# A GEGLU feed-forward kernel whose GELU is computed by one ScalarE activation and one VectorE multiply instead of seven operations

## The chip, the cores and the metric

The kernel runs on one core of a Trainium2 chip. Times are device microseconds (us) of one execution; the *span* in a profile is from the first to the last instruction and is about 2 us shorter than the time. Engines: PE is TensorE, PEld its weight loads, ACT is ScalarE, DVE is VectorE, SP issues most transfers. PSUM is the memory that matmuls accumulate into; a bank is one of its 8 buffers of 128x512 here. The granted clock is the share of TensorE's full clock that the profile records. A run is of the slow state when it took over 1.5% more than the fastest of its kernel; unless a state is named, compared runs are of the fast state.

## The reference

```python
B, S, D, F = 32, 32, 1024, 3584            # bf16; x is 1024 x 1024, the weights 1024 x 3584 and 3584 x 1024
def reference(x, w_gate, w_up, w_down):
    return (gelu_tanh(x @ w_gate) * (x @ w_up)) @ w_down
```

## The kernel before

F is cut into 28 slices `ft` of 128, the 1024 tokens into two blocks of 512. The *first stage* makes, for each of the 56 tiles (128 of F by 512 tokens), a gate and an up accumulation of 8 matmuls each, in one PSUM bank each; all 8 banks rotate. The elementwise work turns each pair of banks into a tile of `gT`. The *second stage* multiplies `gT` by `w_down`: 17 accumulations of 28 matmuls.

```python
FC = 4; KQ = DT // 4                        # DT = 8
pspool = ctx.enter_context(tc.tile_pool(name="psum", bufs=8, space=PSUM))
ework  = ctx.enter_context(tc.tile_pool(name="ework", bufs=3))
...
def mm1(ps, wt, t0, tw, d0=0, d1=DT):       # one accumulation of the first stage
    for dt in range(d0, d1):
        nc.tensor.matmul(ps, lhsT=wt[:, dt, :], rhs=xT[:, dt, t0 : t0 + tw],
                         start=(dt == 0), stop=(dt == DT - 1))

def eltwise(ft, t0, tw, gate_ps, up_ps):    # gelu(g) written as g * sigmoid(g * (C2 + C2A * g * g))
    h = ework.tile(...)
    nc.scalar.activation(h, gate_ps, ACT.Copy)
    sq = ework.tile(...)
    nc.scalar.activation(sq, gate_ps, ACT.Square)
    w = ework.tile(...)
    nc.vector.tensor_scalar(w, sq, _C2A, _C2, ALU.mult, ALU.add)
    z = ework.tile(...)
    nc.vector.tensor_tensor(z, w, h, ALU.mult)
    s = ework.tile(...)
    nc.scalar.activation(s, z, ACT.Sigmoid)
    hu = ework.tile(...)
    nc.vector.tensor_tensor(hu, h, up_ps, ALU.mult)
    nc.vector.tensor_tensor(gT[:, ft, t0 : t0 + tw], hu, s, ALU.mult)
...
# head: the first four tiles are accumulated together, quarter by quarter of D as the weights arrive,
#       so that they hold all 8 banks; then the other 52 tiles one after the other
# second stage: out_ps[128 tokens, 512] = sum over ft of gT[:, ft].T @ wd[:, ft]; VectorE evicts, ScalarE's queue stores
```

Of the kernel before, what the change touches and what calls it, by code (L numbers as in the profile page):

```python
# [8 lines left out]
ACT = mybir.ActivationFunctionType  # L9
ALU = mybir.AluOpType  # L10

_C2 = 2.0 * 0.7978845608028654
_A = 0.044715
_C2A = _C2 * _A
# [3 lines left out]
def kernel(  # L18
# [8 lines left out]
    nc = tc.nc  # L27
    P = nc.NUM_PARTITIONS
    fp32 = mybir.dt.float32
    bf16 = mybir.dt.bfloat16  # L30
# [10 lines left out]
    NB = min(N, MM_N)  # L41
# [20 lines left out]
    ework = ctx.enter_context(tc.tile_pool(name="ework", bufs=3))  # L62
# [5 lines left out]
    gT = gpool.tile([P, FT, N], bf16, name="gT")  # L68
# [55 lines left out]

    def eltwise(ft, t0, tw, gate_ps, up_ps):
        h = ework.tile([P, NB], bf16, name="h", tag="h")[:, :tw]
        nc.scalar.activation(h, gate_ps, ACT.Copy)  # L127
        sq = ework.tile([P, NB], bf16, name="sq", tag="sq")[:, :tw]
        nc.scalar.activation(sq, gate_ps, ACT.Square)  # L129
        w = ework.tile([P, NB], bf16, name="w", tag="w")[:, :tw]  # L130
        nc.vector.tensor_scalar(w, sq, _C2A, _C2, ALU.mult, ALU.add)  # L131
        z = ework.tile([P, NB], bf16, name="z", tag="z")[:, :tw]
        nc.vector.tensor_tensor(z, w, h, ALU.mult)  # L133
        s = ework.tile([P, NB], bf16, name="s", tag="s")[:, :tw]
        nc.scalar.activation(s, z, ACT.Sigmoid)  # L135
        hu = ework.tile([P, NB], bf16, name="hu", tag="hu")[:, :tw]
        nc.vector.tensor_tensor(hu, h, up_ps, ALU.mult)  # L137
        nc.vector.tensor_tensor(gT[:, ft, t0 : t0 + tw], hu, s, ALU.mult)  # L138

    def pair(tw):  # L140
        return (
# [4 lines left out]
    def mm1_and_eltwise(ft, t0, tw):  # L146
        ps = pair(tw)
        for p, wt in zip(ps, weights_of(ft)):
            mm1(p, wt, t0, tw)
        eltwise(ft, t0, tw, *ps)  # L150
# [16 lines left out]
    with tc.manual_schedule(engines={mybir.EngineType.PE}):  # L167
        for _ in range(NWARM):
            nc.tensor.matmul(warm_ps, lhsT=ones_w, rhs=ones_m, start=True, stop=True)  # L169
        for dt in range(KQ):  # L170
            for half in range(2):
                hw = HALF * P
                tp = pspool.tile([P, hw], bf16, name="tp", tag="acc")
                for b in range(HALF):
                    nc.tensor.transpose(  # L175
                        tp[:, b * P : (b + 1) * P],
                        x_nat[:, half * HALF + b, dt * P : (dt + 1) * P],
                        ident,
                    )
                dst = xT[:, dt, half * hw : (half + 1) * hw]  # L180
                if half == 0:
                    nc.vector.tensor_copy(dst, tp)  # L182
                else:
                    nc.scalar.copy(dst, tp)  # L184
        nc.tensor.matmul(warm_ps[:, : NB // 2], lhsT=ones_w, rhs=ones_m[:, : NB // 2], start=True, stop=True)
        head = [pair(NB) for _ in range(FC)]
        for q in range(3):
            for which in (0, 1):
                for dt in range(q * KQ, (q + 1) * KQ):
                    for ft in range(FC):  # L190
                        mm1(head[ft][which], weights_of(ft)[which], 0, NB, dt, dt + 1)
        for ft in range(FC):
            for which in (0, 1):
                mm1(head[ft][which], weights_of(ft)[which], 0, NB, 3 * KQ, DT)
            eltwise(ft, 0, NB, *head[ft])
# [66 lines left out]
```

## Time and profile before

| | before |
|---|---|
| time | 300.71 us (median of 2, 300.66 to 300.75) |
| span of the profiled run | 298.2 us, granted TensorE clock 0.999 |
| PE / DVE / ACT busy | 98% / 37% / 33% |
| rate of matmuls with 512 columns | 216 ns from one to the next, in both stages |

From the profile's page of the kernel before: the busy line and the chain of waits that ended last. Some records of matmuls are missing (1361 of 1387), so PE's true share is nearer 99%.

```profile
PE 292.8 (98%) x1361; PEld 134.4 (45%) x1387; DVE 108.9 (37%) x243; ACT 98.1 (33%) x172; POOL 0.7 (0%) x6
...
PE 96%; DMA 2%; issue 1%; ACTq 0%; DVE 0%
PE out_ps L212 32%; PE up_ps L117 32%; PE gate_ps L117 32%; DMA wu<-in_w_up_dram 2%; ACTq L96 0%; ACTq L80 0%; DVE o_sb L220 0%
```

The chain has no ACT work and no DVE work of the first stage. Its DMA share is one early wait for weights.

The cost groups of the same kernel (busy us in all, mean ns of one, idle time of that engine just before them and what ended it):

```profile
L117 PE MATMUL up_ps<-xT,wu 128*128 128x512 bf16 x440 | 105.6, 379 | 0.5
...
L127 ACT ACTIVATE h<-gate_ps 128x512 bf16<-128x512 f32 x56 | 33.4, 597 | 52.3 <-PE gate_ps L117 51.4
L135 ACT ACTIVATE s<-z 128x512 bf16<-128x512 bf16 x56 | 35.3, 630 | 46.1 <-DVE z L133 46.1
L131 DVE TENSOR_SCALAR w<-sq 128x512 bf16<-128x512 bf16 x56 | 16.5, 295 | 74.6 <-ACT sq L129 74.5
L137 DVE TENSOR_TENSOR hu<-h,up_ps 128x512 bf16<-128x512 bf16 x56 | 38.1, 681 | 12.0 <-ACT h L127 11.9
...
L129 ACT ACTIVATE sq<-gate_ps 128x512 bf16<-128x512 f32 x56 | 33.1, 592 | 0.0
L138 DVE TENSOR_TENSOR gT<-hu,s 128x512 bf16<-128x512 bf16 x56 | 23.8, 426 | 9.9 <-ACT s L135 9.9
L133 DVE TENSOR_TENSOR z<-w,h 128x512 bf16<-128x512 bf16 x56 | 23.8, 425 | 1.8
```

Read the last column by engine. PE has next to no idle time; ACT and DVE have a great deal, and it is PE, or each other, that they wait for. The 379 ns of a matmul is its recorded length, not its pace: matmuls overlap. The pace shows in the timeline, here one tile of the steady first stage (start us, length us, engine, line, idle before):

```profile
186.21 1.89 PE L117 MATMUL up_ps<-xT,wu 128*128 128x512 bf16 x8
186.47 0.60 ACT L127 ACTIVATE h<-gate_ps 128x512 bf16<-128x512 f32 x1 [0.86 <-PE gate_ps L117]
186.97 0.59 ACT L129 ACTIVATE sq<-gate_ps 128x512 bf16<-128x512 f32 x1
187.59 0.29 DVE L131 TENSOR_SCALAR w<-sq 128x512 bf16<-128x512 bf16 x1 [1.52 <-ACT sq L129]
...
187.94 1.89 PE L117 MATMUL gate_ps<-xT,wg 128*128 128x512 bf16 x8
188.26 0.68 DVE L137 TENSOR_TENSOR hu<-h,up_ps 128x512 bf16<-128x512 bf16 x1
188.44 0.63 ACT L135 ACTIVATE s<-z 128x512 bf16<-128x512 bf16 x1 [0.88 <-DVE z L133]
189.10 0.43 DVE L138 TENSOR_TENSOR gT<-hu,s 128x512 bf16<-128x512 bf16 x1 [0.16 <-ACT s L135]
...
189.67 1.89 PE L117 MATMUL up_ps<-xT,wu 128*128 128x512 bf16 x8
```

From 186.21 to 187.94 to 189.67: a group of eight starts every 1.73 us, a tile every 3.45 us, whatever ACT and DVE do in between. The Trainium skill ("TensorE: Matmul & The Clock Gate", "Part 2: What happens when you issue a matmul") gives about 216 ns as the gap between matmuls of 512 columns; 1.73 us / 8 = 216 ns agrees. PE keeps the pace that the page gives, so this is taken as PE's limit.

### The profile page before, as it was taken

Reading aid. Unit: us, or ns where it says so; the run is one execution under the profiler, and the core shown is the slowest. Engines: PE = TensorE matmul, PEld = TensorE weight load, DVE = VectorE, ACT = ScalarE, POOL = GpSimd, SP = SyncE. Lnnn points to the kernel's source line nnn. Section 1 sums busy time; section 2 is a strip of 40 time slices with the busy share of each in tenths; the row PEclk is TensorE's granted clock in tenths of the full one; section 3 lists DMA queues with packets and bytes.
Section 4 is the critical chain, followed back from the end, with each engine's and each line's share of the span. In section 5 each row is a group of like instructions: output and inputs, shape, how many; then the busy total and the mean of one; then the engine's idle time right before and its main releaser. Section 6 shows DMA issues by size and latency. Waiting matters only on the chain.

```text
span 298.2 us, 3467 instructions
## 1 busy us (share of the span) xinstructions
PE 292.8 (98%) x1361; PEld 134.4 (45%) x1387; DVE 108.9 (37%) x243; ACT 98.1 (33%) x172; POOL 0.7 (0%) x6
## 2 busy tenths in 40 slices
PE   8999999999999999999999999999999999999996
PEld 3444444444444444444444444444444444444444
DVE  0067654455554445554445555440010001100111
ACT  2087545544544554544554454530000000000000
POOL 0000000000000000000000000000000000000000
PEclk9999999999999999999999999999999999999999
DMA  7999995090026005300800000000001000100001
GB/s 171 317 295 380 387 363 204 0 281 2 0 78 203 2 0 183 98 2 2 279 4 0 0 0 2 0 0 18 20 18 35 18 20 18 35 20 18 18 19 36
DMA packets 28704, 26.43 MB, mean 89 GB/s; under 512 B 8209, under 2 KB 25105, under 8 KB 28689
## 3 DMA queue, kind: packets, MB, share of 16 engines
q1 hardware_dynamic: 25552, 23.60, 25.1%
q10 hardware_dynamic: 3136, 2.62, 2.8%
q8 instruction: 11, 0.18, 0.2%
q14 instruction: 5, 0.03, 0.0%
HBM read 22.28 MB, written 2.10 MB: 82 GB/s over the span
## 4 chain that ended last, share of the span: by engine, by line
PE 96%; DMA 2%; issue 1%; ACTq 0%; DVE 0%
PE out_ps L212 32%; PE up_ps L117 32%; PE gate_ps L117 32%; DMA wu<-in_w_up_dram 2%; ACTq L96 0%; ACTq L80 0%; DVE o_sb L220 0%
## 5 line engine op out<-in xcount | busy, mean ns | idle before, releaser
L117 PE MATMUL gate_ps<-xT,wg 128*128 128x512 bf16 x438 | 105.6, 379 | 0.7
L117 PE MATMUL up_ps<-xT,wu 128*128 128x512 bf16 x440 | 105.6, 379 | 0.5
L212 PE MATMUL out_ps<-wd,gT 128*128 128x512 bf16 (+2 forms) x468 | 96.5, 366 | 0.4
L212 PEld LDWEIGHTS <-gT 128*128 128x128 bf16 x476 | 45.5, 98 | 51.6
L117 PEld LDWEIGHTS <-wu 128*128 128x128 bf16 x448 | 43.8, 98 | 53.2 <-DMA wu<-in_w_up_dram 0.6
L117 PEld LDWEIGHTS <-wg 128*128 128x128 bf16 x448 | 43.8, 98 | 52.9 <-DMA wg<-in_w_gate_dram 0.3
L127 ACT ACTIVATE h<-gate_ps 128x512 bf16<-128x512 f32 x56 | 33.4, 597 | 52.3 <-PE gate_ps L117 51.4
L135 ACT ACTIVATE s<-z 128x512 bf16<-128x512 bf16 x56 | 35.3, 630 | 46.1 <-DVE z L133 46.1
L131 DVE TENSOR_SCALAR w<-sq 128x512 bf16<-128x512 bf16 x56 | 16.5, 295 | 74.6 <-ACT sq L129 74.5
L137 DVE TENSOR_TENSOR hu<-h,up_ps 128x512 bf16<-128x512 bf16 x56 | 38.1, 681 | 12.0 <-ACT h L127 11.9
L220 DVE CAST o_sb<-out_ps 128x512 bf16<-128x512 f32 (+2 forms) x17 | 11.2, 661 | 84.4 <-PE out_ps L212 79.1
L129 ACT ACTIVATE sq<-gate_ps 128x512 bf16<-128x512 f32 x56 | 33.1, 592 | 0.0
L138 DVE TENSOR_TENSOR gT<-hu,s 128x512 bf16<-128x512 bf16 x56 | 23.8, 426 | 9.9 <-ACT s L135 9.9
L133 DVE TENSOR_TENSOR z<-w,h 128x512 bf16<-128x512 bf16 x56 | 23.8, 425 | 1.8
L169 PE MATMUL warm_ps<-const-bfloat16-1.0 128*128 128x512 bf16 x6 | 2.7, 623 | 0.8 <-PEq L246 0.8
L182 DVE COPY xT<-tp 128x256 bf16<-128x256 bf16 x2 | 0.6, 292 | 4.0 <-PE tp L175 4.0
L184 ACT ACT_TABLE_LOAD x1 | 1.3, 1283 | 2.3 <-issue 2.3
L169 PEld LDWEIGHTS <-const-bfloat16-1.0 128*128 128x128 bf16 x6 | 0.7, 133 | 1.9 <-issue 1.9
L135 ACT ACT_TABLE_LOAD x1 | 1.3, 1283 | 0.0
L175 PEld LDWEIGHTS <-x_nat 128*128 128x128 bf16 x8 | 0.6, 116 | 1.0 <-DMA x_nat<-in_x_dram 0.9
L175 PE MATMUL tp<-ident,x_nat 128*128 128x128 bf16 x8 | 0.8, 266 | 0.0
L184 ACT COPY xT<-tp 128x256 bf16<-128x256 bf16 x2 | 0.6, 374 | 0.6 <-PE tp L175 0.6
(8 smaller groups left out, 1.3 us busy)
## 6 DMA issues: line engine op xcount, KB each, us to landing
wd<-in_w_down_dram SPq DMA_DIRECT2D x7, 1024.0 KB, 13.5
wg<-in_w_gate_dram SPq DMA_DIRECT2D x6, 1024.0 KB, 5.3
wu<-in_w_up_dram SPq DMA_DIRECT2D x6, 1024.0 KB, 6.7
out_dram<-o_sb ACTq DMA_DIRECT2D x15, 128.0 KB, 1.7
wg<-in_w_gate_dram SPq DMA_DIRECT2D x3, 256.0 KB, 3.8
wu<-in_w_up_dram SPq DMA_DIRECT2D x3, 256.0 KB, 4.0
wu<-in_w_up_dram ACTq DMA_DIRECT2D x1, 256.0 KB, 4.8
x_nat<-in_x_dram ACTq DMA_DIRECT2D x1, 128.0 KB, 3.0
```

The source lines that it names most:

```text
L117: nc.tensor.matmul(ps, lhsT=wt[:, dt, :], rhs=xT[:, dt, t0 : t0 + tw], start=(dt == 0), stop=(dt == DT - 1),)
L127: nc.scalar.activation(h, gate_ps, ACT.Copy)
L129: nc.scalar.activation(sq, gate_ps, ACT.Square)
L131: nc.vector.tensor_scalar(w, sq, _C2A, _C2, ALU.mult, ALU.add)
L133: nc.vector.tensor_tensor(z, w, h, ALU.mult)
L135: nc.scalar.activation(s, z, ACT.Sigmoid)
L137: nc.vector.tensor_tensor(hu, h, up_ps, ALU.mult)
L138: nc.vector.tensor_tensor(gT[:, ft, t0 : t0 + tw], hu, s, ALU.mult)
L169: nc.tensor.matmul(warm_ps, lhsT=ones_w, rhs=ones_m, start=True, stop=True)
L184: nc.scalar.copy(dst, tp)
L212: nc.tensor.matmul(out_ps, lhsT=gT[:, ft, tsl], rhs=wd[:, ft, dsl], start=(ft == 0), stop=(ft == FT - 1),)
L220: nc.vector.tensor_copy(o_sb, out_ps)
```

## The change

The intent: the seven operations are one function of the gate, which ScalarE has as a single activation, and the multiply by the up bank can take its result at once.

```diff
     def eltwise(ft, t0, tw, gate_ps, up_ps):
         h = ework.tile([P, NB], bf16, name="h", tag="h")[:, :tw]
-        nc.scalar.activation(h, gate_ps, ACT.Copy)
-        sq = ework.tile([P, NB], bf16, name="sq", tag="sq")[:, :tw]
-        nc.scalar.activation(sq, gate_ps, ACT.Square)
-        ... (w, z: two VectorE operations; s: ACT.Sigmoid; hu: VectorE multiply by up_ps)
-        nc.vector.tensor_tensor(gT[:, ft, t0 : t0 + tw], hu, s, ALU.mult)
+        nc.scalar.activation(h, gate_ps, ACT.Gelu_apprx_tanh)
+        nc.vector.tensor_tensor(gT[:, ft, t0 : t0 + tw], h, up_ps, ALU.mult)
```

## The prediction

> **What bounds the kernel now.** TensorE, from end to end. The page's busy line has PE at 98% of a 298.2 us span, DVE 37%, ACT 33%; the chain of waits that ended last is 96% PE (2% the first weight transfers, none of it the changed elementwise work). Busy PE need not be PE at its peak, so I checked its rate: in that chain, eight matmuls of the first stage take 1.73 us, 216 ns each; in the timeline, 14 blocks of 28 of the second lie between the evictions at 204.54 and 289.15 us, again 216 ns each. The Trainium skill, "TensorE: Matmul & The Clock Gate", "Part 2: What happens when you issue a matmul", gives 216 ns as the back-to-back gap for 512 columns; the trace agrees. The granted clock is 0.999. The rate is the same with ACT and DVE half busy (first stage) and nearly idle (second), so the elementwise work doesn't slow matmuls.
>
> Sum (estimate from these): 4.6 us before the first real matmul + 896 x 216 ns = 193.4 + 420 x 216 ns and a last block in two pieces = 96.8 + about 0.4 of early waits for weights + 3.0 of last eviction and store = 298.2. Nothing in it is elementwise work of the first stage.
>
> **What the change does.** Per tile of 128x512, by the cost groups: ACT Copy 0.597, Square 0.592, Sigmoid 0.630 us become one activation, about 0.6 us (the skill, "ScalarE: Activation LUTs", "What ACT_TABLE_LOAD costs": every function costs the same per element; the three here agree within 7%). DVE 0.295 + 0.425 + 0.681 + 0.426 = 1.83 us become one multiply with a PSUM operand, 0.68 us like the old one by the up bank. Over 56 tiles ACT goes from 98 to about 36 us busy, DVE from 109 to about 50. Table loads stay at two of 1.283 us.
>
> **On the critical path:** about none of it. A tile costs PE 16 x 216 ns = 3.45 us; ACT and DVE spent 1.8 us each. Where it could matter:
> - Head: the first four tiles take all eight banks; the next pair needs the first gate bank at 18.73 us. Copy and Square free it at 17.0, the up bank at 17.23. Afterwards about 16.5 (17.8 if the table load falls in between) and 17.2 to 18.5: still in time.
> - Between the stages: the last gT piece lands at 199.89 us and is needed 27 matmuls after 198.30, at about 204. It will land near 199.1. PE has no gap there already.
> - The tail after the last matmul has none of the changed work.
>
> **Prediction:** 300.6 us, 8 in 10 between 299.6 and 301.6. Faster by over 2%: 1%; within 2%: 98%; slower by over 2%: 1%.
>
> **What would show it.** PE still 98%, about 293 us; eight matmuls still 1.73 us; the second stage still starts near 198.3 us; the gelu 0.58 to 0.66 us; one table load of 1.28 us before the first gelu that PE doesn't wait for; DVE's idle time ends mostly on PE's up bank.
>
> **What would make it wrong.** Another order of matmuls or loads out of the compiler (a PE gap at the head or between stages); a tanh-form gelu of several times a Sigmoid (it binds only past 3.45 us a tile), or its table reloaded often. Lighter ACT and DVE could change the granted clock, but it is at 0.999. A gain would need PE gaps that I failed to see: about 0.4 us are left between matmuls.

## The result, and the profile after

Ratios and intervals in this document are made from fast runs alone; they are not quite the ratios of the medians quoted.

| | before | after |
|---|---|---|
| time, first comparison | 300.71 us (2 runs) | 300.30 us (300.27 to 300.34, 2 runs); ratio 0.9995, 95% interval 0.9976 to 1.0014 |
| time, again with 5 rounds | 300.19 us (299.44 to 300.67, 11 runs) | 300.54 us (299.62 to 300.73, 6 runs); ratio 1.0009, interval 0.9992 to 1.0027 |
| span of the profiled run | 298.2 us | 298.6 us |
| ACT busy | 98.1 us | 36.7 us |
| DVE busy | 108.9 us | 50.3 us |

The results are correct in both. The two comparisons differ in sign and both intervals hold 1: the same time.

From the page of the kernel after, the lines that answer to those above: busy line, chain, and cost groups.

```profile
PE 294.8 (99%) x1387; PEld 135.0 (45%) x1387; DVE 50.3 (17%) x75; ACT 36.7 (12%) x60; POOL 0.7 (0%) x6
...
PE 99%; DVE 0%; issue 0%
...
L117 PE MATMUL up_ps<-xT,wu 128*128 128x512 bf16 x448 | 106.3, 379 | 0.0
...
L128 DVE TENSOR_TENSOR gT<-h,up_ps 128x512 bf16<-128x512 bf16 x56 | 38.5, 688 | 156.6 <-PE up_ps L117 143.7
L127 ACT ACTIVATE h<-gate_ps 128x512 bf16<-128x512 f32 x56 | 33.4, 597 | 158.2 <-PE gate_ps L117 158.2
```

Some 120 us of busy time are gone from two engines (61.4 on ACT, 58.6 on DVE), and all of it turned up as idle time of the same engines: 158 us of ACT's idleness is now ended by a finished gate bank, 144 us of DVE's by a finished up bank. The gelu costs 597 ns, exactly what the Copy of the same bank cost. That agrees with the Trainium skill ("ScalarE: Activation LUTs", "What ACT_TABLE_LOAD costs"), by which all functions cost the same per element.

The steady tile in the timeline of the kernel after:

```profile
186.57 1.89 PE L117 MATMUL up_ps<-xT,wu 128*128 128x512 bf16 x8
186.77 0.60 ACT L127 ACTIVATE h<-gate_ps 128x512 bf16<-128x512 f32 x1 [2.86 <-PE gate_ps L117]
...
188.30 1.89 PE L117 MATMUL gate_ps<-xT,wg 128*128 128x512 bf16 x8
188.57 0.69 DVE L128 TENSOR_TENSOR gT<-h,up_ps 128x512 bf16<-128x512 bf16 x1 [2.76 <-PE up_ps L117]
...
190.03 1.89 PE L117 MATMUL up_ps<-xT,wu 128*128 128x512 bf16 x8
```

186.57, 188.30, 190.03: the groups still start every 1.73 us. Note also how little sooner a tile is finished. Before, `gT` was written 1.6 us after the up bank's last group gave way to the next (187.94 to 189.53); now it takes 1.0 us (188.30 to 189.26). Much of the old chain had run under the up matmuls.

The whole difference between the two profiled spans lies in the first 9 us. The first groups of real matmuls, before and then after:

```profile
4.60 1.89 PE L117 MATMUL gate_ps<-xT,wg 128*128 128x512 bf16 x8
...
6.63 1.90 PE L117 MATMUL up_ps<-xT,wu 128*128 128x512 bf16 x8
...
8.37 1.89 PE L117 MATMUL gate_ps<-xT,wg 128*128 128x512 bf16 x8
```

```profile
4.38 2.78 PE L117 MATMUL gate_ps<-xT,wg 128*128 128x512 bf16 x8
...
7.00 1.89 PE L117 MATMUL up_ps<-xT,wu 128*128 128x512 bf16 x8
...
8.72 1.89 PE L117 MATMUL gate_ps<-xT,wg 128*128 128x512 bf16 x8
```

After, the first group took 2.78 us instead of 1.89, since its first matmuls went at half the pace (0.43 us each); before, PE was at full pace but waited for the up weights. The net is 0.35 us at 8.7 us, and it is carried unchanged to the end. It is a matter of the run, not of the kernel: the same changed kernel, profiled again, took 2.23 us for that group and had a span of 298.0 us, a third profile of it, the one kept for after_again, took 1.89 us and then waited 0.80 us for the up weights, and an experiment with the old elementwise code (quarter_before) had the half pace too. The Trainium skill ("TensorE: Matmul & The Clock Gate", "What's actually happening") says that the clock is released by a free-running window of activity, so that the number of slow matmuls varies from run to run; the varying lengths (2.78, 2.23, 1.89 us) agree, and the window itself was not tested.

### The profile page after: what moved, and what is told of

It reads as the page before. It is cut to its first block, busy times and chain, and to the rows that moved or that the text cites. A ratio compares the mean times of both kernels' runs of the same rounds, so it can differ in the third digit from the quotient of the medians.

```text
span 298.6 us, 3164 instructions
## 1 busy us (share of the span) xinstructions
PE 294.8 (99%) x1387; PEld 135.0 (45%) x1387; DVE 50.3 (17%) x75; ACT 36.7 (12%) x60; POOL 0.7 (0%) x6
## 4 chain that ended last, share of the span: by engine, by line
PE 99%; DVE 0%; issue 0%
PE gate_ps L117 33%; PE out_ps L202 32%; PE up_ps L117 32%; PE warm_ps L159 1%; PE tp L165 0%; DVE o_sb L210 0%; PE warm_ps L175 0%
## 5 line engine op out<-in xcount | busy, mean ns | idle before, releaser
L117 PE MATMUL gate_ps<-xT,wg 128*128 128x512 bf16 x448 | 107.2, 381 | 0.0
L128 DVE TENSOR_TENSOR gT<-h,up_ps 128x512 bf16<-128x512 bf16 x56 | 38.5, 688 | 156.6 <-PE up_ps L117 143.7
L174 ACT ACT_TABLE_LOAD x1 | 1.3, 1283 | 2.3 <-issue 2.3
L127 ACT ACT_TABLE_LOAD x1 | 1.3, 1283 | 0.0
```

Of the source, the lines that this page charges most:

```text
L127: nc.scalar.activation(h, gate_ps, ACT.Gelu_apprx_tanh)
L128: nc.vector.tensor_tensor(gT[:, ft, t0 : t0 + tw], h, up_ps, ALU.mult)
L174: nc.scalar.copy(dst, tp)
```

## The experiments

Theory T: the removed work lay wholly under PE's 3.45 us per tile, and neither slowed the matmuls nor delayed a bank. Rivals: the work saved something that a new cost gave back (R); ACT and DVE traffic slowed the matmuls, or held something else of PE's (contention). All twelve runs follow.

### The changed kernel again

No edit.

> The changed kernel as it stands, with more rounds. Theory T (the removed work lay off the critical path; TensorE is bound by its own rate of 216 ns per matmul): ratio 1.000 to the kernel before, within 0.3%, 300.0 to 301.0 us. Rival R (the removed work did save something, and a new cost at the start gave it back): a clear gain or loss of 0.5 us or more in the median, and a repeated difference in the first 10 us of the trace.

Measured: 300.54 us, ratio 1.0009, interval 0.9992 to 1.0027. No clear gain or loss of 0.5 us appears (the interval runs from 0.24 us faster to 0.81 us slower, so a loss of that size is not excluded), and the start of the trace differs from that of the first profile of the same kernel.

### More elementwise work than before the change, below PE's time

```diff
         nc.vector.tensor_tensor(gT[:, ft, t0 : t0 + tw], h, up_ps, ALU.mult)
+        for _ in range(4): nc.scalar.activation(ja, h, ACT.Gelu_apprx_tanh)     # ja, jd: new tiles, never read
+        for _ in range(5): nc.vector.tensor_tensor(jd, h, h, ALU.mult)
```

> Four useless gelus of h on ACT and five useless multiplies h x h on DVE are added to each tile of the changed kernel: ACT about 2.5 us and DVE 2.4 to 2.8 us per tile, more than the 1.7 us each of the kernel before, but under the 3.45 us that the 16 matmuls of a tile take. Theory T: 300.0 to 301.2 us, same as both kernels within 0.4%, eight matmuls still 1.73 us. A rival, contention (work of ACT and DVE in SBUF and PSUM slows the matmuls, so that the change did give the matmuls something): over 2 us slower, eight matmuls clearly over 1.73 us.

Measured: 300.31 us, ratio 1.0004, interval 0.9991 to 1.0018. The middle of the first stage, 30 to 190 us, of the kernels before and after and of this one (columns: stretch, its length, then busy us with instruction counts for PE, PEld, DVE, ACT, POOL, then granted clock, DMA share, GB/s):

```profile
30.00:190.00 160.00, 159.21 (x728) 72.55 (x742) 81.69 (x187) 79.45 (x140) 0.00 (x0) 1.00 0.29 97
```

```profile
30.00:190.00 160.00, 160.00 (x743) 72.50 (x741) 32.05 (x47) 27.46 (x46) 0.00 (x0) 1.00 0.29 97
```

```profile
30.00:190.00 160.00, 160.00 (x744) 72.53 (x742) 113.24 (x288) 132.25 (x239) 0.00 (x0) 1.00 0.29 98
```

ACT was busy for 79, 27 and 132 of 160 us, and PE loaded 742, 741 and 742 sets of weights in that time (its matmul records are incomplete in the first). This is the direct test of contention: between 17% and 83% of ACT, PE's rate doesn't move. The useless operations read and write SBUF alone; for ACT's and DVE's reads of PSUM, which the change cut from three to two a tile, the test is the first two lines, and half_before against half_after below.

### More elementwise work than PE's time: ScalarE, then VectorE

```diff
+        for _ in range(8): nc.scalar.activation(ja, h, ACT.Gelu_apprx_tanh)     # act_over
```
```diff
+        for _ in range(10): nc.vector.tensor_tensor(jd, h, h, ALU.mult)         # dve_over
```

> Eight useless gelus per tile on ACT, DVE untouched: nine activations at about 0.5 us from start to start, 4.5 us per tile, over the 3.45 us of PE. Theory T: now ACT sets the pace, 56 x about 1.05 us more: 355 to 372 us, ACT over 95% busy in the first stage and PE waiting there for ACT. If elementwise work were hidden by something other than this comparison of time per tile, the time would stay near 300 us or rise otherwise.

Measured: 359.22 us, ratio 1.1974, within the expectation. The pace is 4.65 us per tile (first write of `gT` at 16.9 us, last at 272.4, over 55 steps). In the stretch from 22 to 240 us ACT is busy throughout:

```profile
22.00:240.00 218.00, 177.82 (x762) 76.74 (x761) 30.55 (x48) 218.00 (x424) 0.00 (x0) 0.95 0.26 85
```

> Ten useless multiplies h x h per tile on DVE, ACT untouched: 0.69 + 10 x 0.33 to 0.43 us = 4.0 to 5.0 us per tile, over the 3.45 us of PE. Theory T: DVE sets the pace of the first stage, 335 to 390 us, DVE over 95% busy there. It also says where the limit of DVE lies, as act_over does for ACT.

Measured: 321.18 us, ratio 1.0699; a miss of the size, since at least 335 us was expected. The pace is 3.95 us per tile (16.8 to 234.1 us, 55 steps) and DVE is never idle in the stretch from 22 to 210 us:

```profile
22.00:210.00 188.00, 175.09 (x784) 76.34 (x783) 188.00 (x525) 28.09 (x47) 0.00 (x0) 1.00 0.29 97
```

From the waits of this kernel (us in total, times, longest):

```profile
ACT h L127 <- DVE jd L131: 167.4, 50, 3.4
...
PE gate_ps L117 <- ACT h L127: 13.5, 39, 0.7
```

So DVE held up ACT through the three buffers of `h`, and ACT held up PE. Two things had made my figure too large. A multiply of `h` by itself follows the one before it after 0.34 us, the low end of my range. And PE is ahead of DVE by four tiles, the depth of its eight banks: it started the second stage at 219.2 us while the last `gT` came at 234.1 us, and it lost next to no time there (its weight loads waited 0.6 us for `gT`, once), because the compiled order of this kernel puts matmuls of the next output block in front of those that need the last `gT` tiles: in its trace the last weight load that waits is the 54th of the second stage, in that of the kernel after the 28th.

Together these runs locate the limit: 2.9 us of ACT per tile (fill_under: 132 of 160 us busy, times 3.45) costs nothing, 4.65 us costs 59 us. (55 steps of 1.20 us would be 66; in act_over too PE began its second stage, at 257.3 us, 15 us before the last `gT`.) The old elementwise work stood at about 1.5 us (below).

### Half of the matmuls, old and new elementwise

The first stage contracts over half of D only and loads only those weights.

```diff
+    NQ = 2; DM = NQ * KQ                                # DM = 4 of 8
-    def mm1(ps, wt, t0, tw, d0=0, d1=DT):   ... stop=(dt == DT - 1)
+    def mm1(ps, wt, t0, tw, d0=0, d1=DM):   ... stop=(dt == DM - 1)
     # weight loads 0:DM, and the loops over quarters of D in the head, cut to match
```

> The kernel before with the first stage contracted over only the first half of D (8 matmuls per tile in place of 16, half the weights loaded; the result is wrong on purpose). PE then has 1.73 us per tile, ACT and DVE of the old elementwise about 1.70 and 1.73 us. Theory T: a tie at the limit: 203.6 us (300.3 less 448 x 0.216) to 212 us.

> The changed kernel with the same half contraction (wrong on purpose). Theory T: PE 1.73 us per tile against 0.60 and 0.69: bound by PE, 203 to 205 us, 0 to 8 us less than half_before.

Measured: 203.54 us (202.87 to 204.20) and 203.59 us (202.74 to 204.09): a tie, and 203.6 was the figure for PE alone (half_before is 0.06 us under its stated range, half_after within its own). The stretch from 20 to 90 us of half_before, then of half_after:

```profile
20.00:90.00 70.00, 69.63 (x319) 31.78 (x325) 65.10 (x169) 66.16 (x127) 0.00 (x0) 1.00 0.43 143
```

```profile
20.00:90.00 70.00, 69.63 (x319) 31.73 (x325) 27.53 (x41) 24.53 (x41) 0.00 (x0) 1.00 0.43 146
```

In the first, ACT is busy for 95% of the time and DVE for 93%, and yet PE does the same number of weight loads as in the second. Work that fills 95% of PE's time is still wholly hidden here.

### A quarter of the matmuls, old and new elementwise

The same edit with `NQ = 1`: PE has 4 x 0.216 = 0.86 us of work per tile.

> The kernel before with a quarter of the contraction (4 matmuls per tile, wrong on purpose). PE 0.86 us per tile, the old elementwise 1.70 to 1.85 us. Theory T: bound by ACT and DVE in the first stage, 48 to 55 us above quarter_after: 202 to 212 us, nearly the time of half_before although 224 matmuls fewer than it.

> The changed kernel with a quarter of the contraction (wrong on purpose). Theory T: PE 0.86 us per tile against 0.69 of DVE: still bound by PE, 154 to 157 us (300.3 less 672 x 0.216 = 155.2): the same change that is worth nothing in the whole kernel is then worth some 50 us, 24%. If the removed work were cheap for another reason than PE's cover, the gap between the two quarter kernels would be far smaller.

Measured: 188.79 us (188.50 to 190.61) and 165.21 us (163.71 to 166.15). The change is now worth 23.6 us, so its effect is there when PE's cover is taken away; but both figures missed, one 13 us below its range, the other 8 us above, and the difference is half of the 48 to 55 us expected.

quarter_before was faster because the old elementwise work has a pace of 1.50 us per tile (`gT` written from 10.6 to 93.2 us, 55 steps), not the 1.70 to 1.85 I had added up from the lengths of its operations. In this stretch from 10 to 80 us both engines are full:

```profile
10.00:80.00 70.00, 47.30 (x183) 17.81 (x185) 68.71 (x184) 69.81 (x140) 0.00 (x0) 1.00 0.40 140
```

Three activations take 1.50 us, so one starts every 0.50 us though each is recorded with about 0.6 us. The Trainium skill ("ScalarE: Activation LUTs", "What ACT_TABLE_LOAD costs") says this: back-to-back activations overlap by about 93 ns; here the three lengths add up to 1.82 us, so each overlaps the next by about 0.11 us. I had cited that section and not used the sentence.

quarter_after was slower because of a transfer. From the timeline of its PE:

```profile
19.84 0.59 PE L119 MATMUL up_ps<-xT,wu 128*128 128x512 bf16 x2
27.37 1.04 PE L119 MATMUL gate_ps<-xT,wg 128*128 128x512 bf16 x2 [6.94 <-DMA wg<-in_w_gate_dram]
28.20 1.06 PE L119 MATMUL up_ps<-xT,wu 128*128 128x512 bf16 x2
...
32.29 0.59 PE L119 MATMUL gate_ps<-xT,wg 128*128 128x512 bf16 x2
```

PE waited 6.94 us for the third chunk of gate weights, which SP had queued behind five loads of `w_down` of 1 MB each, and then ran at half pace for some 5 us. (The text below calls it the second chunk; it is the third.) That is 6.9 + about 2.5 = 9.4 us of the 10 missing. This is a flaw of the experiment, so it was mended.

### The quarter kernels with the weights in time, and each half of the change alone

```diff
-    wpool = ctx.enter_context(tc.tile_pool(name="w", bufs=2))
+    wpool = ctx.enter_context(tc.tile_pool(name="w", bufs=NCH))               # a buffer for every chunk
-            wpool.tile([P, DT, FC * P], ...), wpool.tile([P, DT, FC * P], ...)
+            wpool.tile([P, DM, FC * P], ...), wpool.tile([P, DM, FC * P], ...)
```

fed_quarter_act3 adds a useless Copy and Square of the gate bank after the gelu (the change's VectorE half alone); fed_quarter_dve4 adds a scale-and-add and two multiplies in SBUF after the multiply (its ScalarE half alone).

> quarter_before with weight tiles cut to the quarter that is used and one buffer for every chunk of them, so that the loads of w_down no longer go ahead of the later gate and up weights (wrong result on purpose). quarter_before had ACT busy 69.8 and DVE 68.7 of 70 us, 1.50 us per tile; that doesn't change: 186 to 190 us.

> quarter_after fed in the same way. If its miss of 10 us (165.2 against 155.2) was the late second chunk of weights and the half clock after that wait, it goes: 154 to 158 us, PE at 216 ns per matmul throughout, and 30 to 35 us less than fed_quarter_before: 56 tiles x (1.50 - 0.86) = 36 less what the start hides. If the miss had another cause, it stays near 165 us.

> fed_quarter_after with a useless Copy and Square of the gate bank after each gelu: three activations per tile as before the change, one DVE multiply as after it (the DVE half of the change alone). At 1.50 us of ACT per tile: 184 to 190 us, so that the DVE half alone is worth nothing even where elementwise work is exposed. If DVE alone had set the pace of fed_quarter_before: near fed_quarter_after.

> fed_quarter_after with a useless scale-and-add and two useless multiplies in SBUF after each multiply: one activation per tile, four DVE operations of the old forms (the ACT half of the change alone). At 0.65 + 0.20 to 0.33 + 2 x 0.33 = 1.5 to 1.6 us of DVE per tile: 182 to 194 us, the ACT half alone worth next to nothing too. If ACT alone had set the pace: near fed_quarter_after.

| kernel | time (median), us | range of all runs |
|---|---|---|
| fed_quarter_before | 189.48 | 188.29 to 191.00 |
| fed_quarter_act3 | 185.42 | 185.40 to 185.70 |
| fed_quarter_dve4 | 184.05 | 183.84 to 185.82 |
| fed_quarter_after | 155.38 | 155.21 to 157.98 |

The profiled run of fed_quarter_after is slow (157.98 us, low clock in the first slices); the other four, 155.21 to 155.55 us, are fast. The stretch from 15 to 50 us, in the order of the table:

```profile
15.00:50.00 35.00, 23.58 (x90) 8.70 (x91) 34.47 (x94) 34.81 (x71) 0.00 (x0) 1.00 0.66 233
```

```profile
15.00:50.00 35.00, 24.28 (x95) 9.12 (x95) 16.48 (x24) 35.00 (x75) 0.00 (x0) 1.00 0.65 230
```

```profile
15.00:50.00 35.00, 24.72 (x99) 9.52 (x99) 35.00 (x96) 14.33 (x24) 0.00 (x0) 1.00 0.65 230
```

```profile
15.00:50.00 35.00, 34.79 (x160) 15.91 (x163) 27.68 (x42) 24.21 (x41) 0.00 (x0) 1.00 0.65 230
```

Read the full column: both ACT and DVE, ACT alone, DVE alone, and at last PE. fed_quarter_after took 155.38 us where the PE sum said 155.2. So the miss of quarter_after was the late weights with the half pace after it. With PE's cover gone the change is worth 34.1 us (189.48 - 155.38), against 56 x (1.50 - 0.86) = 36 us from the paces. And here each half alone is worth only 4.1 and 5.4 us of these 34.1: two engines stood at the same limit, and relieving one leaves the other. Why both together were still some 4 to 5 us slower than either alone no run takes apart, but the traces show where it lies. The writes of `gT` in fed_quarter_before, fed_quarter_act3 and fed_quarter_dve4 (lengths in ns, then first and last start in us):

```profile
L140 DVE TENSOR_TENSOR gT<-hu,s x56: 415/417/426, 12.8 to 95.3; 128x512 bf16<-128x512 bf16 x56
```

```profile
L133 DVE TENSOR_TENSOR gT<-h,up_ps x56: 686/686/689, 6.9 to 87.5; 128x512 bf16<-128x512 bf16 x56
```

```profile
L130 DVE TENSOR_TENSOR gT<-h,up_ps x56: 675/676/689, 7.7 to 89.0; 128x512 bf16<-128x512 bf16 x56
```

The first tile is finished 5 to 6 us later in fed_quarter_before: its ACT did three Copies and two Squares, and from 10.86 to 12.14 us the table load, before the first Sigmoid, while in the other two the load was over by 6.05 us. After that the paces are close (1.50, 1.47 and 1.48 us). The useless operations of the two halves also have no reader, so no later step waits for their results as it did for those of the old code.

No run points to a version that beats both kernels in full size. PE's own rate accounts for about 290 of 298 us, and what is left is the 4.4 us before the first real matmul and the 3 us after the last; nothing was tried there.

## Why the prediction was right

- **The bound.** "TensorE, from end to end" was right, and the step that carried it was to check the pace from start to start (216 ns in both stages) rather than the busy share. fill_under confirms the conclusion that was drawn from comparing the stages: elementwise work doesn't slow matmuls.
- **The cost.** ACT 36.7 us (about 36 predicted), DVE 50.3 (about 50), gelu 597 ns (about 0.6), multiply 688 ns (0.68), two table loads of 1283 ns. The second came at 4.77 us, while ACT had nothing else to do, not at the first gelu's data.
- **The critical path.** About none of it, as predicted: 300.30 us against 300.6. In the head the first gate bank was free at 16.86 us (16.5 predicted) and the first up bank at 17.58 us (17.2 to 18.5), and PE needed the first at 19.09 us. The second stage started at 198.66 us (198.3 predicted), the shift coming from the start of that run.
- **Small misses.** The last `gT` landed at 199.62 us, 0.3 us sooner than before; I had said near 199.1. Of the 0.5 us between them, 0.36 is the later start of that run; against the start of the second stage it landed 0.63 us sooner than before (1.59 us before, 0.96 after), and 0.79 was forecast. I also gave "1.8 us" per tile to ACT and DVE by adding up lengths; at full load it is 1.50 us. For the prediction this made no difference, since both figures are under 3.45 us; for the experiments it did.
- **The chance of a gain.** That only 0.4 us were left between matmuls was the whole argument against it, and the twelve runs don't contradict it.

## What to carry to other kernels

In these kernels, removing work from an engine gained time only for the part of its pace that exceeded the pace of the engine in front: max(0, 1.50 - PE time per tile) x 56, which is 0 at 3.45 us, 0 at 1.73 us and 36 us at 0.86 us (34.1 measured). Take paces from start to start, for PE as for the others, since lengths overlap. Where two engines stand at the same limit, relieve both or expect little; and the freed 60 us of each engine here are room for other work, not time.

## What the Trainium skill lacked or had wrong

- "TensorE: Matmul & The Clock Gate", "HAM oscillation — how this bites in real kernels", gives as the rule that PE must have no idle gap of more than about 3.4 us. In act_over gaps of 2.22 us between groups were followed by eight matmuls in 2.94 or 3.48 us instead of 1.89 in some cases (not in all), and the granted clock was 0.95 over that stage: shorter gaps can already cost the clock. In the trace kept of that run the clock stood at half for 3.41 us at a time, seven times in the first stage. The page does say elsewhere ("A second HAM failure mode: psum-queue depth-cycling") that frequent short idles bring the throttle back; what it lacks is how short.
- "ScalarE: Activation LUTs", "Table sets: the hidden batching unit", names the tanh form of gelu only as not being in the gelu set. Here `Gelu_apprx_tanh` needed one load of 1283 ns, was issued in place of the one for Sigmoid, and ran at 597 ns for 128x512 from PSUM, the time of a Copy. The load time is as the page has it ("What ACT_TABLE_LOAD costs"), but not the further 1.38 us that it counts for every switch: in the kernel before, the load ran from 18.48 us, right after a Copy that ended at 18.46, and the Sigmoid started at 19.77.
